# Head 0's shift moved from its queries to a bias inside the exps, with two smaller changes of order

## The chip, the cores and the metric

The kernel runs on one core of one Trainium2 chip. The metric is device time in microseconds (us), lower is better; where several executions are quoted, the median stands first and the range behind it.

## The reference

It is one block of a diffusion-style transformer with adaptive layer norms: attention over a cache, then a gated MLP that mixes tokens. The code is condensed. Only the first line of work matters to the front part of the change, the output projection `@ wo` to the other two.

```python
def _A_ref(x, k_cache, v_cache, wq, wo):          # Sq = Sk = 2048, D = 1024, 32 heads of 128
    q = (x @ wq).reshape(B, Sq, H, Dh).transpose(0, 2, 1, 3)
    scores = einsum('bhqd,bhkd->bhqk', q, k_cache) * Dh ** -0.5
    o = einsum('bhqk,bhkd->bhqd', softmax(scores), v_cache)
    return o.transpose(0, 2, 1, 3).reshape(B, Sq, H * Dh) @ wo

mod = (silu(c) @ w_mod).reshape(1, 6, 1, -1)      # c is (1, 1024), w_mod is (1024, 6144)
sa, ca, ga, sb, cb, gb = mod[:, 0], ..., mod[:, 5]
h = layernorm(x) * (1 + ca) + sa                   # scale ca, shift sa
x = x + ga * _A_ref(h, k_cache, v_cache, wq, wo)
h = layernorm(x) * (1 + cb) + sb
x = x + gb * _B_ref(h, ...)                        # the MLP; not touched by the change
```

Everything arrives in bf16. The shift `sa` enters the queries as one constant vector per head, `sa @ wq`.

## The kernel before

The kernel is long and already tuned: one instruction stream per engine, ordered by hand. Three places matter.

**1. The front.** Attention can start when the first queries exist. For heads 0 and 1 the kernel doesn't modulate the normalised rows: it folds the scale `1 + ca` into the weights (`wqs`), multiplies the plain normalised rows (`xnT`) by these, and adds the shift's product (`q_add`) when VectorE copies the queries out of PSUM. So the first copy waits for the shift. `mod_products(n)` multiplies a 1 MB chunk of `w_mod` by silu(c); chunks 2 and 3 give the scale, 0 and 1 the shift. `emit_s(g)` computes the scores of key block `kb` with 128 keys on the partitions and 1024 queries along the free axis.

```python
    c_sb = early.tile([KD, P], BF16, name="c_sb")
    nc.sync.dma_start(c_sb[:], c.rearrange("o (kc p) -> (o kc) p", p=P))     # first load of all
    # ... cut ...
    def keep_busy(n):                       # products of zeros, 512 columns wide
        zps = qa_ps("zps", [P, 512])
        for _ in range(n):
            nc.tensor.matmul(zps[:], zeros[:, 0:P], zeros[:], start=True, stop=True)

    def query_shift():
        qs = qa_ps("qs", [P, 2])
        for h in range(2):
            for dc in range(KD):
                nc.tensor.matmul(qs[:, h:h + 1], wq_g[0][:, dc, h * DH:(h + 1) * DH],
                                 shift[:, dc:dc + 1], start=(dc == 0), stop=(dc == KD - 1))
        nc.vector.tensor_copy(out=q_add[:], in_=qs[:])
    # ... cut ...
    silu()
    # ... cut: statistics, norm, transposes ...
    mod_products(2, qb_ps)
    mod_products(3)
    # ... cut ...
    turn(3, (0, 1))           # the last transposes, copied out by VectorE and ScalarE
    k_late()
    mod_products(0, qb_ps)
    mod_columns(0)
    # ... cut ...
    outs = []
    first = q_work(0, 0, bank_ps, outs)     # 16 products of head 0's first 1024 queries
    for fn, _ in first[:8]:
        fn()
    mod_products(1, qb_ps)
    mod_columns(1)
    for fn, _ in first[8:12]:
        fn()
    query_shift()
    for fn, _ in first[12:]:
        fn()
    for fn in outs:                          # the two copies that add q_add
        fn()
    emit_s(0)
    emit_s(1)
```

**2. The end of attention.** One half (one head, 1024 queries) takes 16 steps. In the last half the output projection's operands are loaded (`load_heads`, token group 0, then group 1), and the row sums of the half before are turned into reciprocals (`finish_here`), written to memory in four pieces (`spread`), read back broadcast (`load_rec`) and multiplied in (`normalise`). All of these transfers are issued by SyncE, in program order.

```python
        if final:
            if kb == 0:
                # ... cut ...
                load_heads(0, 1)
                load_heads(1, 0)
                load_heads(1, 1)
            elif kb in (4, 6, 8, 10):
                wo_sum(2, (kb - 4) // 2)
            elif kb == 13:
                normalise(i - 1)
        # ... cut ...
        nc.scalar.activation(pt_tiles[g], s_tiles.pop(g)[:], ACT.Exp, scale=SCALE)
        # ... cut ...
        if i > 0:
            # ... cut: two other tables for the earlier halves; that of the final half:
            work = {3: finish_here, 6: load_rec}.get(kb)
```

**3. The last token tile.** In the output projection each finished tile of 128 tokens is normalised `n` blocks later; `after(2, end)` means two. The last tile is normalised on VectorE (`centre`), the others on ScalarE.

```python
        def end():
            hb = scratch("hb", [P, D], FP16)
            (centre_act if ti < NT - 1 else centre)(x1[:, :], st, hb[:])
            after(2, lambda: nc.sync.dma_start(h2_dram[ti * P:(ti + 1) * P, :], hb[:]))
        after(2, end)
```

The softmax here doesn't subtract the row's maximum and nothing guards it: scores larger than these inputs give would overflow.

## Time and profile before

| | before |
|---|---|
| time, 3 runs | 1769.86 us (1768.88 to 1770.56) |
| TensorE busy | 98% of the span |
| start of the first exp | 31.57 us |
| attention's main loop | 31.5 to about 1120 us |
| output projection and MLP | about 1138 us to the end |

The profile's page says what bounds the kernel in one line: the chain that ended last, by engine.

```profile
PE 89%; DVE 6%; DMA 2%; issue 1%; ACT 1%; SPq 0%; POOL 0%; DVEq 0%; ACTq 0%; POOLq 0%
```

The windows view gives busy time by stretch. Its columns are: window, its length, then the busy time (and instruction count) of PE, PEld, DVE, ACT and POOL, then the granted TensorE clock, the DMA share and GB/s. First the front as a whole, two slices of it, and attention:

```profile
0.00:31.50 31.50, 19.86 (x250) 14.96 (x254) 18.86 (x59) 16.22 (x21) 6.29 (x14) 0.89 1.02 312
17.00:20.00 3.00, 1.83 (x24) 1.15 (x22) 2.57 (x9) 1.94 (x5) 0.98 (x2) 0.71 1.06 361
20.00:23.00 3.00, 3.00 (x26) 2.72 (x27) 1.69 (x6) 1.97 (x2) 0.40 (x1) 0.50 1.09 349
...
31.50:1116.00 1084.50, 1077.29 (x5170) 491.80 (x5270) 964.45 (x1252) 1004.90 (x1009) 9.54 (x8) 1.00 0.52 137
```

In attention TensorE is busy for 1077.29 of 1084.50 us: a change there can win time only where TensorE waits. In the front it is busy for 19.86 of 31.50 us, with DMA full (1.02).

The front in the timeline view (columns: start, duration in us, engine, line, operation, output<-inputs, shape; in brackets the idle time before it and what ended it):

```profile
20.79 1.91 PE L286 MATMUL k_ps<-identity,first_rows 128*128 128x128 bf16 x16
...
25.50 1.89 PE L380 MATMUL qps<-xnT,first_rows 128*128 128x512 bf16 x7
...
29.66 1.44 DVE L363 TENSOR_SCALAR qT<-qps,q_add 128x512 bf16<-128x512 f32 x2
31.16 0.81 PE L484 MATMUL sps<-qT,kT 128*128 128x512 bf16 x3 [0.31 <-DVE qT L363]
31.57 3.81 ACT L812 ACTIVATE pt<-sps 128x1024 bf16<-128x1024 f32 x4 [4.03 <-PE sps L484]
```

The two copies that add the shift (L363) run one after the other on VectorE, 1.44 us, and the first score's second half waits for them.

The end of attention in the same view, SyncE's issues (SPq) with VectorE and TensorE:

```profile
1116.17 9.23 SPq L653 DMA_DIRECT2D h_slots<-oT_dram  x6
...
1121.83 0.21 DVE L592 STREAM_TRANSPOSE turned<-rec 128x32 f32<-128x32 f32 x1
...
1125.44 2.56 SPq L594 DMA_DIRECT2D rec_dram<-turned  x4
...
1131.93 0.35 SPq L600 DMA_DIRECT2D rbc<-rec_dram  x1
...
1136.75 1.23 DVE L638 TENSOR_TENSOR s_slots<-ou,rbc 128x1024 bf16<-128x1024 f32 x1 [4.53 <-DMA rbc<-rec_dram]
...
1139.77 3.61 PE L935 MATMUL a<-wo,h_slots 128*128 128x512 bf16 x16 [2.45 <-DVE wq_t L826]
...
1154.06 1.02 PE L935 MATMUL b<-wo_t_11489,s_slots 128*128 128x512 f16 x4
...
1155.19 1.02 PE L935 MATMUL b<-wo_t_11491,s_slots 128*128 128x512 f16 x4
```

Six head loads keep SyncE issuing for 9.23 us. The reciprocals are ready at 1121.83 + 0.21 = 1122.04 us but their write is issued at 1125.44; everything behind it is late, VectorE stands idle 4.53 us, then TensorE 2.45 us. After that VectorE has a backlog: the groups of four products start 1155.19 − 1154.06 = 1.13 us apart.

The last token tile:

```profile
1335.88 0.55 DVE L156 TENSOR_SCALAR hb<-x_in,mv,rstd 128x1024 f16<-128x1024 bf16 x1 [0.73 <-POOL rstd L145]
1336.35 0.62 DVE L983 TENSOR_TENSOR sum<-c,snap 128x448 f32<-128x448 f32 x1
...
1338.06 0.92 PE L935 MATMUL a<-w_12681,hs_12655 128*128 128x448 f16 x4 [1.43 <-ACT snap L978]
```

VectorE waits for the rstd and normalises first; the sum, ScalarE's copy and then TensorE (1.43 us idle) come behind it.

### The profile page before, as it was taken

The numbers are of one execution on the slowest core, as the hardware profiler recorded it, in microseconds if no ns is written. First come the engines' busy times: TensorE is split into PE (matmuls) and PEld (weight loads), VectorE is DVE, ScalarE is ACT, GpSimd is POOL, SyncE is SP. The second block draws the span as 40 slices with busy tenths as digits, with TensorE's granted clock in tenths as the row PEclk, the third lists the DMA queues.
The fourth block names the chain that finished last, engine by engine and source line by source line (L and its number), as shares of the span: only waits on it lengthen the run. The fifth ranks groups of instructions, "written<-read, shape, count | busy, mean of one in ns | idle before, by whom it ended". The sixth has DMA issues, their size and how long they took to land.

```text
span 1767.5 us, 23664 instructions
## 1 busy us (share of the span) xinstructions
PE 1736.4 (98%) x8439; PEld 801.1 (45%) x8556; DVE 1488.6 (84%) x2245; ACT 1298.2 (73%) x1527; POOL 30.5 (2%) x39
## 2 busy tenths in 40 slices
PE   7999999999999999999999999999999999999999
PEld 4444444444444444444444444444444444444444
DVE  6898898898988899998999988896679789775894
ACT  6998889999999999999999999611235666734610
POOL 1000000000000000000000000000000000000000
PEclk9999999999999999999999999999999999999999
DMA  8566356646544633554633564645757364554312
GB/s 250 132 155 145 89 143 166 151 126 159 155 123 134 170 103 101 144 151 129 166 109 96 142 184 128 164 125 158 186 158 206 101 167 114 181 145 139 90 48 72
DMA packets 445335, 247.75 MB, mean 140 GB/s; under 512 B 289312, under 2 KB 406560, under 8 KB 445216
## 3 DMA queue, kind: packets, MB, share of 16 engines
q1 hardware_dynamic: 445216, 246.23, 51.9%
q8 instruction: 67, 1.10, 0.3%
q14 instruction: 52, 0.43, 0.1%
HBM read 144.18 MB, written 52.71 MB: 111 GB/s over the span
## 4 chain that ended last, share of the span: by engine, by line
PE 89%; DVE 6%; DMA 2%; issue 1%; ACT 1%; SPq 0%; POOL 0%; DVEq 0%; ACTq 0%; POOLq 0%
PE ops L750 24%; PE sps L484 23%; PE a L935 15%; PE b L935 8%; PE qa L465 4%; PE qps L380 4%; PE c L935 4%; PE qb L465 3%; PE bo L1537 2%; ACT pt L812 1%; DVE sum L983 1%; DMA wm<-in_w_mod_dram 1%; PE mps L198 0%; PE a_11200 L935 0%; PE a L1615 0%
## 5 line engine op out<-in xcount | busy, mean ns | idle before, releaser
L812 ACT ACTIVATE pt<-sps 128x1024 bf16<-128x1024 f32 x1024 | 1020.7, 1024 | 84.9 <-PE sps L484 38.5
L484 PE MATMUL sps<-qT,kT 128*128 128x512 bf16 x1993 | 597.0, 379 | 3.5 <-ACT pt L812 2.1
L750 PE MATMUL ops<-pt,v_sb 128*128 128x512 bf16 x2017 | 593.5, 379 | 3.7
L484 PEld LDWEIGHTS <-kT 128*128 128x128 bf16 x2048 | 199.4, 98 | 248.1 <-issue 16.4
L750 PEld LDWEIGHTS <-v_sb 128*128 128x128 bf16 x2048 | 200.1, 98 | 241.9
L978 ACT ACTIVATE snap<-a 128x512 f32<-128x512 f32 (+1 forms) x111 | 60.9, 565 | 113.6 <-PE a L935 103.2
L826 DVE COPY ou<-ops 128x512 f32<-128x512 f32 x126 | 81.2, 686 | 32.5 <-PE ops L750 29.7
L935 PEld LDWEIGHTS <-h_slots 128*128 128x128 f16 (+1 forms) x680 | 66.3, 98 | 82.4 <-issue 2.5
L380 PE MATMUL qps<-h1T,wq_t 128*128 128x512 bf16 x279 | 94.3, 379 | 0.3
L983 DVE TENSOR_TENSOR sum<-b,snap 128x512 f32<-128x512 f32 (+1 forms) x76 | 50.1, 660 | 48.4 <-PE b L935 28.7
L1386 ACT ACTIVATE zr<-zr,z_nm,z_rs 128x256 f16<-128x256 f16 x82 | 41.1, 586 | 66.4 <-PE bo L1537 47.1
L638 DVE TENSOR_TENSOR oT<-ou,rbc 128x1024 bf16<-128x1024 f32 x62 | 75.3, 1215 | 0.6 <-DMA rbc<-rec_dram 0.6
L450 DVE COPY tx<-qa 128x512 f32<-128x512 f32 x66 | 45.5, 689 | 32.2 <-PE qa L465 32.2
L616 DVE TENSOR_REDUCE den<-pT 128x8 f32<-128x1024 bf16 x54 | 63.9, 1183 | 0.0
L465 PE MATMUL qa<-h1s,wq_t 128*128 128x512 f16 x176 | 63.1, 379 | 0.3
L935 PEld LDWEIGHTS <-s_slots 128*128 128x128 f16 (+1 forms) x400 | 39.0, 98 | 49.0 <-issue 2.0
L465 PEld LDWEIGHTS <-wq_t 128*128 128x128 bf16 (+1 forms) x352 | 34.4, 98 | 41.5
L935 PEld LDWEIGHTS <-wq_t 128*128 128x128 f16 (+1 forms) x344 | 33.7, 98 | 38.4 <-DMA wq_t<-oT_dram 0.2
L145 POOL TENSOR_TENSOR rstd<-var,neg_half 128x1 f32<-128x1 f32 x30 | 25.1, 836 | 1306.0 <-DVE var L143 1258.9
L445 DVE TENSOR_TENSOR qT<-qb,tx 128x512 bf16<-128x512 f32 x66 | 45.2, 685 | 0.7
L380 PEld LDWEIGHTS <-wq_t 128*128 128x128 bf16 x288 | 28.0, 98 | 33.2 <-issue 0.6
L465 PEld LDWEIGHTS <-tx 128*128 128x128 f16 x264 | 25.8, 98 | 31.2
(930 smaller groups left out, 2553.6 us busy)
## 6 DMA issues: line engine op xcount, KB each, us to landing
rbc<-rec_dram SPq DMA_DIRECT2D x63, 512.0 KB
v_sb<-in_A_v_cache_dram SPq DMA_DIRECT2D x40, 512.0 KB
oT_dram<-oT SPq DMA_DIRECT2D x62, 256.0 KB
sums_dram<-pacc SPq DMA_DIRECT2D x54, 256.0 KB
wm<-in_w_mod_dram SPq DMA_DIRECT2D x12, 1024.0 KB
wq_t<-in_A_wq_dram SPq DMA_DIRECT2D x7, 1024.0 KB
h_slots<-oT_dram SPq DMA_DIRECT2D x12, 512.0 KB
zr<-z_dram SPq DMA_DIRECT2D x11, 512.0 KB
```

The lines of the kernel that those rows point to most:

```text
L380: nc.tensor.matmul(box["ps"][:], weights[:, dc, hc:hc + DH], src[:, dc, q0:q0 + 512], start=(n == 0), stop=(n == KD - 1))
L450: nc.vector.tensor_copy(out=x if m == 6 else su, in_=a)
L465: nc.tensor.matmul(box["b" if m in (2, 7, 4) else "a"][:], *operand(m, dc), start=(m in (1, 2, 7) and dc == 0), stop=(dc == 3), skip_group ...
L484: nc.tensor.matmul(sps[:, j * 512:(j + 1) * 512], kts[h][:, kb * P:(kb + 1) * P], qts[(h, qh)][:, j * 512:(j + 1) * 512], start=True, stop ...
L616: nc.vector.tensor_reduce(out=den[:], in_=state[i]["pT"][:], op=ALU.add, axis=mybir.AxisListType.X)
L638: nc.vector.tensor_mul(out=oT, in0=state[i]["ou"][:], in1=state[i]["rbc"][:])
L750: nc.tensor.matmul(o_ps[j][:], vs[halves[i][0]][:, kb, :], pt_tiles[g][:, j * 512:(j + 1) * 512], start=(kb == 0), stop=(kb == NKB - 1))
L812: nc.scalar.activation(pt_tiles[g], s_tiles.pop(g)[:], ACT.Exp, scale=SCALE)
L826: nc.vector.tensor_copy(out=ou[:, j * 512:(j + 1) * 512], in_=o_ps[j][:])
L935: nc.tensor.matmul(self.ps[self.BANK[n]], a, b, start=(n in (1, 2, 7) and k == 0), stop=(k == len(lhs) - 1), skip_group_check=True)
L978: nc.scalar.activation(t, ps, ACT.Copy)
L983: nc.vector.tensor_add(out=t, in0=ps, in1=snap)
```

## The change

The front: a query's score against a key is (q + s)·k = q·k + s·k, and s·k depends on the key alone. Keys lie on the partitions of the score tile, so s·k can be the bias of the exp, one number per partition. Head 0's queries then need no shift. The shift's product is split into a bf16 part and a bf16 remainder so that nothing is lost. In return each of head 0's first 16 exps carries a bias, 32 small key products and a small copy are added, the order of the front's products changes, one query copy goes to ScalarE, and `c` is loaded behind two tiles of x. The second part moves the last half's group-1 head loads from step 0 to steps 7 and 9, behind the reciprocals. The third defers the last tile's normalisation by one block.

```diff
-    nc.sync.dma_start(c_sb[:], c.rearrange("o (kc p) -> (o kc) p", p=P))
 ...
     for ti in range(8):
         nc.sync.dma_start(xg[ti // 2][:, ti % 2], x_dram[:, ti, :])
+        if ti == 1:
+            nc.sync.dma_start(c_sb[:], c.rearrange("o (kc p) -> (o kc) p", p=P))
 ... query_shift(h, dcs) now takes one head and a range of chunks; for head 0 it ends with
+            hi, lo = q_add0[:, 0:1], q_add0[:, 1:2]
+            nc.vector.tensor_copy(out=hi, in_=qs[0][:])
+            nc.vector.tensor_sub(out=lo, in0=qs[0][:], in1=hi)
 ...
+    def key_shift(k0, k1, new_ps):
+        ks = new_ps("ks", [P, k1 - k0])
+        for k in range(k0, k1):
+            for t in range(2):
+                nc.tensor.matmul(ks[:, k - k0:k - k0 + 1], kts[0][:, k * P:(k + 1) * P],
+                                 q_add0[:, t:t + 1], start=(t == 0), stop=(t == 1),
+                                 skip_group_check=True)
+        nc.scalar.activation(key_add[:, k0:k1], ks[:], ACT.Copy, scale=SCALE)
 ...
-    turn(3, (0, 1))
-    k_late()
-    mod_products(0, qb_ps)
-    mod_columns(0)
+    x_late = turn(3, True)
 ... in q_work's copies:
+            elif h == 0 and plain and not j:
+                nc.scalar.activation(qts[h, qh][:, sl], box["ps"][:], ACT.Copy)
 ...
-    first = q_work(0, 0, bank_ps, outs)
+    first = q_work(0, 0, (qa_ps, bank_ps))
     for fn, _ in first[:8]:
         fn()
+    x_late()
+    k_late()
+    mod_products(0, qb_ps)
+    mod_columns(0)
+    for fn, _ in first[8:]:
+        fn()
+    query_shift(0, range(4))
     mod_products(1, qb_ps)
     mod_columns(1)
-    for fn, _ in first[8:12]:
-        fn()
-    query_shift()
-    for fn, _ in first[12:]:
-        fn()
-    for fn in outs:
-        fn()
+    query_shift(0, range(4, KD))
     emit_s(0)
+    key_shift(0, 2, qb_ps)
     emit_s(1)
+    query_shift(1, range(KD))
 ...
                 load_heads(0, 1)
-                load_heads(1, 0)
-                load_heads(1, 1)
             elif kb in (4, 6, 8, 10):
                 wo_sum(2, (kb - 4) // 2)
+            elif kb in (7, 9):
+                load_heads(1, (kb - 7) // 2)
 ...
-        nc.scalar.activation(pt_tiles[g], s_tiles.pop(g)[:], ACT.Exp, scale=SCALE)
+        bias = {"bias": key_add[:, kb:kb + 1]} if i == 0 else {}
+        nc.scalar.activation(pt_tiles[g], s_tiles.pop(g)[:], ACT.Exp, scale=SCALE, **bias)
+        if g == 0:
+            key_shift(2, NKB, qb_ps)
 ...
-        after(2, end)
+        after(2 if ti < NT - 1 else 3, end)
```

More of the change, by code (lines that the diff above doesn't have):

```diff
@@ L215 @@
     shift = early.tile([P, KD], BF16, name="shift")
-    q_add = early.tile([P, 2], FP32, name="q_add")
+    q_add = early.tile([P, 1], FP32, name="q_add")
+    q_add0 = early.tile([P, 2], BF16, name="q_add0")
+    key_add = early.tile([P, NKB], FP32, name="key_add")
     def scale_wq(j):
@@ L226, in scale_wq, with query_shift @@
                                         op0=ALU.mult)
-    def query_shift():
-        qs = qa_ps("qs", [P, 2])
-        for h in range(2):
-            for dc in range(KD):
-                nc.tensor.matmul(qs[:, h:h + 1], wq_g[0][:, dc, h * DH:(h + 1) * DH],
-                                 shift[:, dc:dc + 1], start=(dc == 0), stop=(dc == KD - 1))
-        nc.vector.tensor_copy(out=q_add[:], in_=qs[:])
+    qs = []
+    def query_shift(h, dcs):
+        if dcs[0] == 0:
+            qs[:] = [qa_ps("qs", [P, 1])]
+        for dc in dcs:
+            nc.tensor.matmul(qs[0][:], wq_g[0][:, dc, h * DH:(h + 1) * DH],
+                             shift[:, dc:dc + 1], start=(dc == 0), stop=(dc == KD - 1))
+        if dcs[-1] < KD - 1:
+            return
+        if h:
+            nc.vector.tensor_copy(out=q_add[:], in_=qs[0][:])
+        else:
+            hi, lo = q_add0[:, 0:1], q_add0[:, 1:2]
[9 more added lines that the diff above has]
+        nc.scalar.activation(key_add[:, k0:k1], ks[:], ACT.Copy, scale=SCALE)
     row = {}
@@ L263, in finish_act, with turn @@
         row[ti] = (mv, rstd)
-    def turn(j, evacuate=(2,)):
+    def turn(j, late=False):
         hps = wide_ps("hps", [P, KD, 2, P], BF16)
@@ L270, in turn, with out @@
                                     xg[j][:, t, dc * P:(dc + 1) * P], identity[:])
-        for eng in evacuate:
-            dcs = {2: slice(0, KD), 0: slice(0, 4), 1: slice(4, KD)}[eng]
-            dst = xnT[:, dcs, j * 256:(j + 1) * 256]
-            src = hps[:, dcs].rearrange("p d t k -> p d (t k)")
-            if eng:
+        def out():
+            dst = xnT[:, :, j * 256:(j + 1) * 256]
+            src = hps[:].rearrange("p d t k -> p d (t k)")
+            if late:
+                nc.vector.tensor_copy(out=dst, in_=src)
+            else:
                 nc.scalar.activation(dst, src, ACT.Copy)
-            else:
-                nc.vector.tensor_copy(out=dst, in_=src)
+        if late:
+            return out
+        out()
     def dve(ti):
@@ L351, with q_work @@
     tags = [qa_ps, qb_ps]
-    def q_work(h, qh, new_ps=None, outs=None):
+    def q_work(h, qh, new_ps=None):
         plain = h < 2 and qh == 0
@@ L361, in out @@
             sl = slice(j * 512, (j + 1) * 512)
-            if plain:
+            if h == 1 and plain:
                 nc.vector.tensor_scalar_add(out=qts[h, qh][:, sl], in0=box["ps"][:],
-                                            scalar1=q_add[:, h:h + 1])
+                                            scalar1=q_add[:])
+            elif h == 0 and plain and not j:
+                nc.scalar.activation(qts[h, qh][:, sl], box["ps"][:], ACT.Copy)
             else:
@@ L369, in q_work @@
             box = {}
-            tag = new_ps or tags[j]
+            tag = (new_ps or tags)[j]
             def one(n, j=j, box=box, tag=tag):
@@ L382, in one @@
                                  start=(n == 0), stop=(n == KD - 1))
-                if n == KD - 1 and outs is None:
+                if n == KD - 1:
                     out(j, box)
-                elif n == KD - 1:
-                    outs.append(lambda: out(j, box))
             for n in range(KD):
@@ L490 @@
     nc.sync.dma_start(wq_g[1][:], wq_v[:, :, 512:1024])
-    outs = []
-    first = q_work(0, 0, bank_ps, outs)
+    first = q_work(0, 0, (qa_ps, bank_ps))
     for fn, _ in first[:8]:
         fn()
+    x_late()
[5 more added lines that the diff above has]
+    query_shift(0, range(4))
     mod_products(1, qb_ps)
     mod_columns(1)
-    for fn, _ in first[8:12]:
-        fn()
-    query_shift()
-    for fn, _ in first[12:]:
-        fn()
-    for fn in outs:
-        fn()
+    query_shift(0, range(4, KD))
     emit_s(0)
+    key_shift(0, 2, qb_ps)
     emit_s(1)
+    query_shift(1, range(KD))
     state = {}
```

## The prediction

> **What bounds the kernel now.** The chain that ended last is 89% TensorE; in the windows, TensorE is busy 1077 of 1084.5 us in attention (31.5 to 1116 us). Time can be won only where TensorE waits. The diff touches three such places.
>
> 1. Front (first exp at 31.57 us). DMA is saturated from about 2 us on; x loads are issued behind c's (0.74 to 1.20 us), and the chain runs through the second modulation chunk, landing at 16.29. From 19.96 TensorE is nearly continuous until 30.3; then two VectorE query copies (1.44 us) delay the first score's second half to 31.16.
> 2. End of attention. In the timeline six head loads hold SyncE's queue from 1116.17 to 1125.40, though the reciprocals were ready at 1122.04. They are written 1125.44 to 1131.79, the broadcast lands at 1136.73, and VectorE sits idle 4.53 us before normalising. TensorE then idles about 2.3 us (1137.3 to 1139.8), and from 1154 to 1158.3 is paced at 1.13 us per four matmuls instead of 0.86 by VectorE's backlog (another 1.2).
> 3. Last token tile. VectorE waits 0.73 us for the rstd, then normalises (0.55) before the next sum; ScalarE follows, and TensorE waits 1.43 us at 1338.06.
>
> **Costs.**
> - c behind two x tiles: x starts 0.46 us earlier, so the 16.29 landing should too: −0.4 at the front's gate.
> - Head 0's queries no longer wait for the shift; one copy goes to ScalarE; turn 3 is evicted in one VectorE copy (estimate 1.35 us from 0.69 for half), hidden behind eight matmuls. But the first exp now waits for shift products, two small VectorE operations (0.16 each), key products and a 0.2 us ScalarE copy. First exp at about 31.5: nearly no gain.
> - 32 small key products at about 31 ns (32 such take 0.95 to 1.0 us). Most fit the wait during exp 0 (0.67 us before), but the 14-column bias copy delays exp 1 by about 0.5 us. Bias operand: the Trainium skill ("ScalarE: Activation LUTs", "What ACT_TABLE_LOAD costs") says each per-partition pointer operand adds about 93 ns; this trace agrees (256-column activation: 404, 495 with one, 586 ns with two). So 16 exps go from 1024 to about 1115 ns; TensorE's step is 1.08 us, their overlapped spacing about 1.05: hidden. Front net: about +0.3 us (−0.7 to +0.9).
> - Head loads of group 1 behind the reciprocals: these are written from about 1122.1, the broadcast lands about 1130, before the multiply's turn at 1132.2. The 2 MB follow, at about 290 GB/s landing by about 1135, needed at 1137.5 and 1141. Stall and backlog vanish: −3.2 us (−2 to −4).
> - Last tile: the sum goes ahead of the normalisation; TensorE's 1.43 us wait falls to about 0.4: −0.8 us (−0.2 to −1.2).
>
> Downstream is TensorE-paced, so these should persist: 1769.86 + 0.3 − 3.2 − 0.8 = about 1766.2 us, range 1763.6 to 1768.4. Faster by over 2%: 0.01; within 2%: 0.98; slower: 0.01.
>
> **What would show it.** VectorE's 4.5 us wait for the broadcast gone; reciprocal writes near 1122; TensorE's wait on the ou copies gone; group 1's first products not waiting for head loads; four-matmul groups back at 0.86. First exp within 0.4 us of 31.57; exps of the first half near 1115 ns; a TensorE wait of some 0.4 us on exp 1. TensorE's wait at the last tile under 0.5 us. Second modulation chunk's products about 0.45 us earlier.
>
> **What would make it wrong.** Late head loads putting a new wait on the first output products; the bias exps pacing the first half; key products delaying exp 1 by more; the last tile's later store delaying transposed loads, giving its gain back; changed buffer slots adding waits.

## The result, and the profile after

The changed kernel took 1765.04 us (1763.56 to 1766.74, 4 runs) against 1770.07 us (1768.88 to 1770.56, 4 runs) for the kernel before, run beside it. The ratio is 0.9973 (95% interval 0.9956 to 0.9990). A ratio here and below is the mean time of one kernel's fast runs over that of the other's of the same rounds, so it is not quite the ratio of the medians that are quoted. The gain is about 4.8 us (0.0027 of 1770), well under 2%.

The chain of the changed kernel, from its page:

```profile
PE 86%; DVE 7%; DMA 3%; ACT 2%; issue 1%; SPq 1%; DVEq 0%; ACTq 0%
```

The front, windows view, changed kernel:

```profile
0.00:31.50 31.50, 20.83 (x288) 14.59 (x292) 19.39 (x60) 18.66 (x26) 6.29 (x14) 0.92 0.99 316
17.00:20.00 3.00, 2.69 (x18) 1.81 (x18) 2.83 (x9) 1.70 (x4) 1.38 (x2) 0.52 1.07 385
20.00:23.00 3.00, 2.95 (x42) 2.41 (x41) 1.93 (x6) 2.70 (x2) 0.00 (x0) 1.00 1.08 381
26.00:28.00 2.00, 1.67 (x44) 1.33 (x44) 0.99 (x4) 0.00 (x0) 0.00 (x0) 1.00 1.10 336
...
30.00:32.00 2.00, 2.00 (x6) 0.77 (x6) 0.29 (x1) 2.00 (x3) 0.00 (x0) 0.54 1.14 176
```

The half-clock stretch lies elsewhere: the slice from 20 to 23 us now has full speed, while the one from 30 to 32 us has 0.54 and six products fill it. The timeline shows both:

```profile
20.10 1.06 PE L312 MATMUL k_ps<-identity,first_rows 128*128 128x128 bf16 x16
22.10 1.89 PE L405 MATMUL qps<-xnT,first_rows 128*128 128x512 bf16 x7
...
28.79 1.11 ACT L838 ACTIVATE pt<-sps,key_add 128x1024 bf16<-128x1024 f32 x1
...
29.96 0.86 PE L507 MATMUL sps<-qT,kT 128*128 128x512 bf16 x2
30.61 1.49 PE L405 MATMUL qps<-xnT,first_rows 128*128 128x512 bf16 x3
```

The 16 key transposes took 1.06 us instead of 1.91. The first exp starts at 28.79 us, 2.78 us earlier than before. But three products of 512 columns then take 1.49 us (0.81 in the timeline of before at 33.07 us), and by the fifth exp only 1.00 us of the 2.78 is left.

The groups view by form shows the cost of the bias operand in the changed kernel (count, busy us, mean ns of one, idle before):

```profile
L838 ACT ACTIVATE pt<-sps,key_add 128x1024 bf16<-128x1024 f32 x16 | 17.4, 1114 | 1.8 <-PE sps L507 0.9 <-remote 0.9
```

The end of attention, timeline of the changed kernel:

```profile
1123.36 0.21 DVE L617 STREAM_TRANSPOSE turned<-rec 128x32 f32<-128x32 f32 x1
...
1123.60 1.52 SPq L619 DMA_DIRECT2D rec_dram<-turned  x4
1126.49 0.35 SPq L625 DMA_DIRECT2D rbc<-rec_dram  x1
1126.89 4.53 SPq L678 DMA_DIRECT2D h_slots<-oT_dram  x3
...
1133.68 1.22 DVE L663 TENSOR_TENSOR s_slots<-ou,rbc 128x1024 bf16<-128x1024 f32 x1
...
1138.91 3.62 PE L963 MATMUL a<-wo,h_slots 128*128 128x512 bf16 x16
...
1152.93 1.03 PE L963 MATMUL b<-wo_t_11529,s_slots 128*128 128x512 f16 x4
...
1153.79 1.03 PE L963 MATMUL b<-wo_t_11531,s_slots 128*128 128x512 f16 x4
```

The reciprocals are written 0.03 us after they are ready (1123.36 + 0.21 = 1123.57), the normalisation and the first projection product have no wait, and the groups of four are 0.86 us apart again.

The last tile, timeline of the changed kernel:

```profile
1333.05 0.61 DVE L1011 TENSOR_TENSOR sum<-c,snap 128x448 f32<-128x448 f32 x1
...
1334.91 0.53 DVE L157 TENSOR_SCALAR hb<-x_in,mv,rstd 128x1024 f16<-128x1024 bf16 x1
1334.75 0.92 PE L963 MATMUL a<-w_12721,hs_12695 128*128 128x448 f16 x4 [0.15 <-ACT snap L1006]
```

The sum now goes first and TensorE's wait is 0.15 us instead of 1.43.

To see where time was gained or lost I subtracted, in each trace, the start of the n-th exp (or of the n-th ScalarE copy of the projection) from that in the trace of before. The instructions of these two lines come in the same order in all the kernels. All numbers in us, minus is earlier; exps are counted from 1 here (the prediction counts from 0, so its exp 1 is exp 2 here). "Attention" is what was lost between exp 5 and exp 1013 of 1024, "end" what was gained from there to the seventh copy (at 1184 us before), "last tile" what was gained from the 25th copy (1328 us) to the 34th (1348 us).

| kernel | first exp at | exp 1 | exp 5 | attention | end | last tile |
|---|---|---|---|---|---|---|
| before | 31.57 | | | | | |
| after | 28.79 | −2.78 | −1.00 | +2.54 | −3.48 | −0.78 |
| again | 30.06 | −1.51 | −1.30 | +1.44 | −3.48 | −0.78 |
| front_only | 28.16 | −3.41 | −3.20 | +0.40 | −0.53 | 0.00 |
| loads_only | 31.41 | −0.16 | −0.16 | −0.05 | −3.48 | 0.00 |
| tile_only | 31.10 | −0.46 | −0.46 | +0.26 | +0.36 | −0.78 |
| c_only | 30.38 | −1.19 | −1.18 | −0.06 | −0.39 | −0.01 |
| bias_only | 28.32 | −3.24 | −1.58 | +0.87 | −0.27 | 0.00 |
| loads_tile | 30.79 | −0.78 | −0.78 | −0.06 | −3.47 | −0.77 |
| warm | 28.38 | −3.19 | −1.52 | +0.17 | −3.48 | −0.78 |
| warm_old | 30.53 | −1.04 | −1.04 | +0.40 | −3.48 | −0.79 |
| warm_new | 28.09 | −3.48 | −3.27 | +0.75 | −3.48 | −0.77 |
| warm_wide | 28.91 | −2.66 | −1.80 | +0.02 | −3.48 | −0.78 |
| loads_pool | 30.00 | −1.57 | −1.57 | +0.15 | −2.45 | 0.00 |

One trace is one execution. But "end" repeats to 0.01 us in the eight traces with the moved loads, and "last tile" to 0.02 in the eight with the tile's part; in the five without that part it is zero. The front doesn't repeat: five traces (before, loads_only, tile_only, loads_tile, loads_pool) have the front of the kernel before, and their first exp comes anywhere from 30.00 to 31.57 us. The trace of before, from which everything is subtracted, has the latest, so the columns "exp 1" and "exp 5" flatter the other kernels. Stretches between the columns wander too: from the seventh copy to the 25th by −0.3 to +1.25 us, in three traces by about +1.2.

### The profile page after: what moved, and what is told of

Same layout as the page of the kernel before. It is cut to its first block, busy times and chain, and to the rows that moved or that the text cites. A ratio compares the mean times of both kernels' runs of the same rounds, so it can differ in the third digit from the quotient of the medians.

```text
span 1764.6 us, 23738 instructions
## 1 busy us (share of the span) xinstructions
PE 1737.2 (98%) x8471; PEld 800.6 (45%) x8588; DVE 1488.3 (84%) x2246; ACT 1298.2 (74%) x1529; POOL 30.5 (2%) x39
## 4 chain that ended last, share of the span: by engine, by line
PE 86%; DVE 7%; DMA 3%; ACT 2%; issue 1%; SPq 1%; DVEq 0%; ACTq 0%
PE ops L775 22%; PE sps L507 22%; PE a L963 15%; PE b L963 8%; PE c L963 4%; PE qps L405 4%; PE qa L488 4%; PE qb L488 3%; PE bo L1565 2%; ACT pt L838 1%; DMA rec_dram<-turned 1%; DMA rbc<-rec_dram 1%; DVE sum L1011 1%; DMA wm<-in_w_mod_dram 1%; PE a_11236 L963 1%
## 5 line engine op out<-in xcount | busy, mean ns | idle before, releaser
L838 ACT ACTIVATE pt<-sps 128x1024 bf16<-128x1024 f32 x1008 | 1003.8, 1024 | 83.0 <-PE sps L507 32.9
L146 POOL TENSOR_TENSOR rstd<-var,neg_half 128x1 f32<-128x1 f32 x30 | 25.1, 836 | 1304.1 <-DVE var L144 1278.2
```

## The experiments

My theory after the result: the three parts act separately, the loads give about 3.5 us, the tile 0.8, and the front's value depends on where TensorE's clock is halved. The first rival: the parts interact, or the front's earlier start carries much of the gain. A second question was why the queue mattered. All twelve kernels gave correct results. Each ratio is against the kernel before in the same rounds (5 rounds; 3 for loads_pool).

| kernel | median us (range) | before, same rounds | ratio (95%) |
|---|---|---|---|
| again | 1764.57 (1763.68–1767.35) | 1769.16 | 0.9974 (0.9961–0.9988) |
| front_only | 1769.37 (1767.16–1770.89) | 1769.16 | 0.9998 (0.9986–1.0011) |
| loads_only | 1765.48 (1763.77–1767.11) | 1769.16 | 0.9978 (0.9965–0.9990) |
| tile_only | 1768.66 (1767.75–1770.10) | 1769.16 | 0.9997 (0.9984–1.0009) |
| c_only | 1768.02 (1767.23–1768.81) | 1768.80 | 0.9997 (0.9985–1.0010) |
| bias_only | 1769.03 (1765.78–1769.47) | 1768.80 | 0.9999 (0.9986–1.0011) |
| loads_tile | 1764.36 (1764.21–1766.35) | 1768.80 | 0.9979 (0.9966–0.9992) |
| warm | 1764.44 (1764.05–1765.09) | 1768.80 | 0.9977 (0.9963–0.9991) |
| warm_old | 1764.61 (1763.95–1765.43) | 1768.56 | 0.9975 (0.9961–0.9988) |
| warm_new | 1762.72 (1762.26–1763.66) | 1768.56 | 0.9964 (0.9952–0.9977) |
| warm_wide | 1763.45 (1763.03–1765.44) | 1768.56 | 0.9971 (0.9958–0.9983) |
| loads_pool | 1766.56 (1766.23–1770.41) | 1768.56 | 0.9990 (0.9977–1.0004) |

### again: the changed kernel once more

No edit; a control, beside which the single parts are read. It ran on chip 2, as front_only, loads_only and tile_only did; the later runs were on chip 0.

> The changed kernel once more, as a control. Theory (three parts that add up, and two lotteries): the time is about 4 to 5 us below the kernel before; the stall of 2.9 us on the broadcast reciprocals in half 15, and the two 3.4 us windows of half clock at 16.5 and 30.1 us in the first profile, need not come back, because they are luck of the run: then the first-exp-to-last-exp distance is within 0.5 us of the kernel before's instead of 4.3 us longer. Rival (the change causes both): the profile shows the half-15 wait again at about 3 us and again a half-clock window that starts within 2 us after the first exp.

Measured: 1764.57 us, ratio 0.9974. The result repeats. Its trace has another clock pattern than the first: the first exp comes at 30.06 us. Its clock column is a trap:

```profile
17.00:20.00 3.00, 2.69 (x16) 1.74 (x16) 2.83 (x10) 1.70 (x4) 1.37 (x2) 1.00 1.07 385
```

It reads 1.00, but the first clock record of this trace comes only at 22.46 us, and the key transposes at 20.34 us took the slow 1.91 us. Before the first record the column says nothing.

### front_only: the front alone

```diff
 # the changed kernel, with
+                load_heads(1, 0)
+                load_heads(1, 1)
-            elif kb in (7, 9):
-                load_heads(1, (kb - 7) // 2)
-        after(2 if ti < NT - 1 else 3, end)
+        after(2, end)
```

> The front alone (c's load moved, key bias, reordered first queries), head loads and last tile as before. Theory: the first exp comes 0.5 to 3 us earlier (by how much depends on which window of the front gets half clock), 1 us is left after exp 5, and the time is 0 to 1.5 us below the kernel before. Rival (the front is where the change wins): 3 us or more below.

Measured: ratio 0.9998, first exp at 28.16 us. This trace has no half-clock stretch after 14.9 us. The front's gain is then 3.41 us at exp 1, and 3.20 at exp 5: the cost that I had put at the second exp (key products and the bias copy) is 0.29 us there at full clock, and 0.21 by exp 5. Of the 3.20 us, 2.90 are still there at the last copies of the projection. That execution was the fastest of the five (1767.16; the others 1768.32 to 1770.89), so the mean shows next to nothing of it.

### loads_only: the head loads alone

```diff
 # the kernel before, with
-                load_heads(1, 0)
-                load_heads(1, 1)
+            elif kb in (7, 9):
+                load_heads(1, (kb - 7) // 2)
```

> The group-1 head loads behind the last half's reciprocals alone. Theory: VectorE's 4.5 us wait for the broadcast is gone, first output blocks start about 3.3 us earlier against the last exp, and the time is 2.5 to 4 us below the kernel before. Rival (the gain needs the front's shift or other buffer slots, or is given back in the output projection): under 1.5 us.

Measured: ratio 0.9978, which is 3.9 us, with 1.8 to 6.2 in its interval. In the trace the step at the end of attention is −3.48 us, nothing else moves by more than 0.2. This part alone is most of the change.

### tile_only: the last tile alone

```diff
 # the kernel before, with
-        after(2, end)
+        after(2 if ti < NT - 1 else 3, end)
```

> The last tile's normalisation one block later alone. Theory: TensorE's 1.43 us wait at the last tile falls below 0.4 us and 0.8 us is left at the end; the time is 0.3 to 1.2 us below the kernel before. Rival (the later store of the last rows delays the transposed loads and gives it back): the block two later waits, and the time is within 0.2 us.

Measured: ratio 0.9997, about 0.5 us and not to be told from nothing. In the trace the copy at 1337 us comes 1.29 us earlier relative to the one at 1328 us, and 0.46 us are given back by the one at 1340 us; at 1348 us 0.78 are left, as in the seven other traces with this part. Something else is visible. TensorE's wait at 1137 to 1140 us, still there in this kernel, was followed by 3.4 us of half clock from 1140.4 us, and between the first copy (at 1139 us) and the fourth (1154 us) 1.68 us were lost. That window is in none of the other thirteen traces, the kernel before's included, which has the same wait.

### c_only: c behind two tiles of x, alone

```diff
 # the kernel before, with
-    nc.sync.dma_start(c_sb[:], ...)        # ahead of x
+        if ti == 1:
+            nc.sync.dma_start(c_sb[:], ...)
```

> c's load behind two x tiles alone. Theory: x and everything behind it on the saturated DMA lands 0.46 us earlier, so the second modulation chunk's products start about 0.5 us earlier and the first exp 0.3 to 0.6 us earlier, if the windows of half clock lie as in the kernel before; the whole time is 0 to 0.6 us lower, inside its noise. Rival (c's move is what frees the front of half clock): no or one half-clock window between 14 and 25 us instead of two, first exp 1.5 us or more earlier.

Measured: ratio 0.9997; first exp 1.19 us earlier in the trace, with the clock's half-speed stretch starting at 15.8 us instead of 18.2. The prediction put 0.4 us here, and the products of the second modulation chunk (the trace's second `mps` group) did start 0.41 us earlier, at 15.93 instead of 16.34. But loads_tile, which loads c first, has them at 15.56, and loads_pool, with the old front unchanged, has its first exp at 30.00: neither gain can be put down to the move. Nothing of it can be told from zero in time.

### bias_only: the front without c's move

```diff
 # front_only, with c's load back at the head of the queue
```

> The key bias and the reordered first queries alone, c's load first as before. Theory of the prediction: at the same clock the first exp comes about 0.3 us later or equal (31.5 to 32.0 us), exp 1 is 0.4 us late, exp 4 on within 0.5 us of the kernel before. Rival (the reordering takes waits out of the front for real): first exp 0.8 us or more earlier at the same clock windows. In time: within 1 us of the kernel before either way.

Measured: ratio 0.9999. First exp at 28.32 us, but here a half-clock stretch of 3.4 us starts at 29.3 us, as in the changed kernel's first trace, and 3.24 us of gain shrink to 1.58 by exp 5. So the first exp's gain doesn't come from c's move; and the loss behind it goes with the clock, not with the bias: front_only has the same exps with a bias and lost 0.2.

### loads_tile: the change without the front

```diff
 # the kernel before, with the edits of loads_only and tile_only
```

> The whole change without its front. Theory (the front's gain is within the noise of clock and DMA, the other two parts are the result): 4.0 to 5.0 us below the kernel before, within 1 us of the whole change. Rival (the front is worth its 1 us and more): 1.3 us or more slower than the whole change's 4.6 us.

Measured: ratio 0.9979, where the whole change has 0.9973 and 0.9974. The difference, 0.0005 to 0.0006, would make the front worth about 1 us; with half-widths of some 0.0013 (2.3 us) on each it can't be told from zero. The three single parts sum to (1 − 0.9978) + (1 − 0.9997) + (1 − 0.9998) = 0.0027, the whole change's 0.0026 to 0.0027. They don't interact noticeably.

### warm: keep TensorE busy early

If the clock decides the front, wide products of zeros early in it should move it. The kernel has a helper for that.

```diff
 # the changed kernel, with
+    keep_busy(6)
     silu()
+    keep_busy(7)
```

> The changed kernel with 13 more idle-time matmuls on zeros (6 before the turn of c, 7 behind it), meant to have full clock before the first transposes. Theory (half clock in the front's windows decides when the first exp comes): no half-clock window between about 8 and 30 us, first exp at 28.5 us or earlier in this profile, and 0.5 to 2 us below the whole change's 4.6 us gain. Rival (the front is bound by the loads, not by TensorE's clock): first exp within 0.3 us of the second profile of the changed kernel (30.06), time as the changed kernel's.

Measured: ratio 0.9977. The trace still has two half-clock stretches, from 15.7 and from 29.4 us, and the profile of the first five exps is that of bias_only. This edit didn't reach its aim: between the two modulation chunks of the scale TensorE still stood idle.

### warm_old and warm_new: both fronts at full clock

A third block of zero products goes into that gap. warm_old has the old order of the front (and all else of the change, c's move too), warm_new the new one. My theory at this point said that at equal clock the new order is worth at most about half a microsecond; the rival said that the order itself is worth more.

```diff
 # both: warm's two calls, and
     mod_products(2, qb_ps)
+    keep_busy(5)
     mod_products(3)
```

> Everything but the key bias and the new order of the first queries (head loads, last tile and c's move as in the change), plus idle-time matmuls on zeros in three places of the front, so that its clock is full. Together with the next run it compares the two orders of the first queries at the same clock. Theory (the new order is worth little: at equal clock the first exp is at most 0.5 us later here, and exp 4 within 0.3 us, because the key bias gives back what the order wins): time within 0.5 us of the next run or lower. Rival (the order is worth 1 us or more, and is hidden by half clock in the other runs): exp 4 at least 1 us later than in the next run, time about 1 us higher.

> The whole change plus the same zero matmuls in the same three places. Theory of the clock (a window in which TensorE runs few wide products is followed by one at half clock): no half-clock window from 9 to 29 us, and one at about 29 to 33 us again when a window boundary lies near 29.3 us, because the window before holds mostly one-column products; exps 2 to 4 then lose 1.1 us or more, else under 0.3. First exp at 27.5 to 28.3 us. Time 5 to 6 us below the kernel before.

Measured: warm_old 1764.61 us, ratio 0.9975; warm_new 1762.72 us, ratio 0.9964. The traces have no half-clock stretch that matters (warm_old one at 9.1 us, warm_new none). The first exp comes at 30.53 and 28.09 us, exp 5 at −1.04 and −3.27. My theory fell. The timeline of warm_old shows what I had missed (the second and third line are chunks 0 and 1, the shift):

```profile
20.27 1.06 PE L287 MATMUL k_ps<-identity,first_rows 128*128 128x128 bf16 x16
22.87 0.95 PE L199 MATMUL mps<-scT,wm 128*128 128x1 bf16 x32 [0.44 <-DMA wm<-in_w_mod_dram]
...
26.17 0.95 PE L199 MATMUL mps<-scT,wm 128*128 128x1 bf16 x32 [0.60 <-DMA wm<-in_w_mod_dram]
```

With the clock at full speed the old order reaches both chunks of the shift before they have landed, and waits 0.44 + 0.60 = 1.04 us. The waits view of warm_old (15 to 34 us; total us, number, longest) counts a third wait, the longest:

```profile
PE mps L199 <- DMA wm<-in_w_mod_dram: 1.8, 3, 0.8
```

That one, 0.75 us at 16.19 us, is for a chunk of the scale. It lies ahead of the key transposes, in a part that both orders share.

warm_new puts the wide query products, which need nothing that is still on its way, ahead of these chunks:

```profile
19.39 1.06 PE L312 MATMUL k_ps<-identity,first_rows 128*128 128x128 bf16 x16
21.40 1.89 PE L408 MATMUL qps<-xnT,first_rows 128*128 128x512 bf16 x7
23.12 0.94 PE L199 MATMUL mps<-scT,wm 128*128 128x1 bf16 x32
25.75 0.94 PE L199 MATMUL mps<-scT,wm 128*128 128x1 bf16 x32
```

None of its products waits for the modulation weights from here on. Of the 2.2 us between the two at exp 5, 20.27 − 19.39 = 0.88 exist already at the key transposes, which stand in the same order in both kernels, and are the luck of one execution; about 1.35 come after. In the ratios the two kernels are 0.0011 apart, about 1.9 us, with intervals that overlap; but each of these compares with the kernel before. Compared directly, in the same rounds on the same chip, all five executions of warm_new (1762.26 to 1763.66 us) lie below all five of warm_old (1763.95 to 1765.43), and the means differ by 1.83 us (my 95% interval from these ten times: 1.1 to 2.6). So with the zero products in place the new front is worth something like that in time.

warm_new is also the fastest of all kernels here: 5.8 us under before in the medians of the same rounds, 6.4 in the mean ratio, against 4.6 in the mean ratio for the changed kernel in again. That it is faster than the changed kernel isn't shown: the two ran in other rounds and on other chips, and the intervals overlap. Nearest to a test is warm, on the same chip in earlier rounds, whose five executions (from 1764.05 us) all lie above warm_new's.

### warm_wide: wide products among the one-column ones

In three traces (after, bias_only, warm) a half-clock stretch begins 0.96 to 1.36 us after the first exp, just behind the front's one-column products (modulation, shift, key products). If such products don't keep the clock up, six wide products of zeros among them should.

```diff
 # warm_new, with keep_busy(n, new_ps=qa_ps) and
     mod_products(1, qb_ps)
+    keep_busy(3, bank_ps)
 ...
     emit_s(1)
+    keep_busy(3, bank_ps)
     query_shift(1, range(KD))
```

> As the run before it, with six more wide zero matmuls in the stretch of one-column products (three behind the second shift chunk, three behind the second score), which cost up to 1.3 us of TensorE's time there. Theory: the half-clock window behind it is gone, exps 2 to 4 lose under 0.3 us; first exp 0.3 to 0.7 us later than in the run before. Rival (the window at 30 us comes from something else, such as the wait on the first exps): it is there still.

Measured: 1763.45 us, ratio 0.9971, 0.7 us slower than warm_new in the medians. Between exp 1 and exp 2 it loses 0.94 us, where warm_new loses 0.28; the difference is about what three of the added products take (0.65 us from their start to the next product's). There was no half-clock stretch behind the first exp, but there was none in warm_new either, so the run can't tell whether they prevented one. It gives no sign that they pay.

### loads_pool: other queue, same transfers in flight

Was it SyncE's queue that held the reciprocals back, or the bytes of the head loads?

```diff
 # the kernel before, with
-                load_heads(1, 0)
-                load_heads(1, 1)
+                load_heads(1, 0, nc.gpsimd)     # issued by GpSimd
+                load_heads(1, 1, nc.gpsimd)
```

> The kernel before with the four group-1 head loads issued at the same place of the program but by GpSimd instead of SyncE. Theory (the loads blocked the queue's issuing, so the reciprocals could not be written): the reciprocals are written from about 1122, within 0.3 us of their being ready, VectorE's wait for the broadcast is under 1 us although the same bytes are in flight, and the time falls by 2.5 to 4 us. Rival (bandwidth: 2 MB in flight delay the reciprocals and their broadcast): the writes are issued at 1122 but the broadcast still lands after 1134, VectorE waits 2 us or more, time falls under 1.5 us.

Measured: 1766.56 us, ratio 0.9990 (0.9977 to 1.0004), in time not to be told from zero, and −2.45 us at the end of attention in the trace. The timeline of loads_pool:

```profile
1107.46 3.79 POOL L653 DMA_DIRECT2D h_slots<-oT_dram  x4 [973.26 <-PE qps L380]
...
1120.40 0.21 DVE L592 STREAM_TRANSPOSE turned<-rec 128x32 f32<-128x32 f32 x1
...
1120.68 3.26 SPq L594 DMA_DIRECT2D rec_dram<-turned  x4
...
1128.44 0.35 SPq L600 DMA_DIRECT2D rbc<-rec_dram  x1
...
1132.90 1.22 DVE L638 TENSOR_TENSOR s_slots<-ou,rbc 128x1024 bf16<-128x1024 f32 x1
```

The queue is free, so the reciprocals go out 0.07 us after they are ready (1120.40 + 0.21 = 1120.61), and the last normalisation doesn't wait. That is the queue's part. But from the write's issue to the broadcast's it takes 1128.44 − 1120.68 = 7.76 us; in loads_only, with group 1's loads not yet issued, the same two stand at 1121.86 and 1124.73, 2.87 us apart, and the DMA moves 44 GB/s in between, against 216 here. In the kernel before it was the same: 1131.93 − 1125.44 = 6.49 us, at 226 GB/s. So there too the reciprocals lost about as much behind the bytes (3.6 us) as behind the queue (3.40 us). And the normalisation of the half before waited 2.09 us for its own broadcast. That is the bytes' part: GpSimd, which had little else to do, issued these loads at 1107.46 us, about 9 us before SyncE began with its own in the kernel before, and they were in flight at the same time as these transfers. The Trainium skill ("DMA: Bandwidth & Descriptors", "Issuing engines are not separate DMA queues") says that transfers started by different engines run on the same 16 DMA engines and interleave, and that a second issuer saves only sequencer time. This trace agrees. So both counted: freeing the queue brought 2.45 of the 3.48 us, and only issuing the loads later brought all of it.

## Why the prediction was right or wrong

**The total was right.** 1766.2 us with a range of 1763.6 to 1768.4; measured 1765.04 in the result and 1764.57 in again. The predicted gain of 3.7 us was 1 us too small. Two of its three terms were right; the third, the front, had the wrong sign in the traces, and it is luck that it was too small to move the total out of the range.

**The head loads: right in size, and in mechanism but for one part.** "−3.2 us (−2 to −4)": the traces give −3.47 or −3.48 us in all eight that have this part, the time of loads_only 3.9. Each sign came: the write at the moment the reciprocals were ready, VectorE's 4.53 us and TensorE's 2.45 us gone, the groups of four back from 1.13 to 0.86 us. The prediction saw the queue: SyncE's stream was held in order, 9.23 us by six loads. It didn't name the bytes in flight, which loads_pool shows to count as well; moving the loads later removes both.

**The last tile: right.** "−0.8 us (−0.2 to −1.2)": in all eight traces with this part 1.28 or 1.29 us are gained and 0.45 or 0.46 given back at the next copies, and 0.77 to 0.79 remain. TensorE's wait went from 1.43 to 0.15 us (predicted: to about 0.4). The giving back was named as a risk through the later store; I didn't trace what causes it. In time the part is too small to be seen (0.9997).

**The bias operand: right.** Predicted 1115 ns for the 16 exps; measured 1114, against 1024 without. This is 90 ns for one pointer operand, where the Trainium skill ("ScalarE: Activation LUTs", "What ACT_TABLE_LOAD costs") has about 93. That it would be hidden behind TensorE was right as well: in front_only the gain is −3.20 us at exp 5 and still at exp 16.

**The front: wrong in mechanism, and small enough not to matter.** The step that failed is "First exp at about 31.5: nearly no gain", and with it "Front net: about +0.3 us". In the traces with the new front and without added zero products the first exp came at 28.16 to 30.06 us. Two things were missed:

1. I added up durations of one trace as if they were fixed. At half clock the sum holds, as far as one pair of traces shows: c_only (old order) and again (new order) both have slow key transposes (1.91 us) and full clock from about 22.5 us on; from the first key transpose to the fifth exp both take 14.01 us. At full clock it doesn't: the old order takes 13.90 (loads_pool) and 14.33 us (warm_old), the new one 12.98 in both traces without a later stretch (front_only, warm_new). The durations between 18.2 and 25.1 us in before were taken at half clock: 16 key transposes take 1.91 us there and 1.06 at full clock. The stretch moves from execution to execution. The Trainium skill ("TensorE: Matmul & The Clock Gate", "What's actually happening") says that the clock is set by windows of 3413 ns that run freely, halved after an idle window. The short clock records of these traces are 3.413, 6.827 and 10.240 us long and start elsewhere each time, which agrees with the windows. Whether the window must be idle this case leaves open: in after TensorE was busy, as the profile counts it, for 3.01 of the 3.41 us before 30.15 us, and half clock followed; if the rule holds, products of one column, most of those in that window, don't count. The windows view of before showed 0.50 in the slice from 20 to 23 us, before I predicted.
2. I counted what the new order stops waiting for (the shift) but not what TensorE itself waits for: the modulation weights. At half clock the two chunks of the shift had always landed in time, which hid the wait. At full clock the old order waits for them, 1.04 us in warm_old and 0.59 in loads_pool, and the new one does not.

The predicted loss at the second exp, "the 14-column bias copy delays exp 1 by about 0.5 us", was 0.29 us at full clock. Where the loss is larger (1.78 us in after, 1.66 in bias_only, 1.67 in warm, from exp 1 to exp 5) a half-clock stretch begins at 29.3 to 30.2 us.

In time the front of the change as it stands is not firm: front_only is at 0.9998 (0.9986 to 1.0011), so it is worth 0.4 us by itself and about 1 us as the difference of the whole and loads_tile, and the predicted loss of 0.3 us is inside both intervals. It is the traces that refute the step, and in time the pair warm_old and warm_new, 1.83 us apart, at the clock that the zero products bring. That half clock costs time fits the list of executions too: of the 27 of the kernel before that ran beside the experiments, the 20 with a mean clock of 0.999 or 1.000 took 1768.6 us on average, the 7 with 0.997 or 0.998 took 1770.2. (That mean counts the time before the first clock record as full speed.)

**What stays open.**
- Whether one-column products fail to keep the clock up. In the trace of after TensorE was busy for 1.67 of 2.00 us from 26 to 28 us, most of its products having one column, and the stretch from 30.1 us was at half speed all the same. Three traces fit, and the four new-front traces without such a stretch had their boundary elsewhere in relation to the first exp, if the boundaries are carried on in steps of 3.413 us; but warm_wide, made to test it, couldn't.
- Why kernels with the new front lose more later in attention: +0.40, +0.87, +2.54, +1.44, +0.17, +0.75 and +0.02 us in seven traces (mean 0.9) against +0.1 on average in six with the old. In the first trace of the changed kernel 1.9 of 2.54 us arise between exps 225 and 257, where VectorE waits 2.90 us for a broadcast; again waits 0.74 us there. Such waits of VectorE for transfers (over 0.1 us each) between exps 5 and 1013 sum to 4.1 to 11.0 us in six of the seven traces (1.1 in warm_wide, which loses 0.02) and to 0.8 to 2.7 us in five of the six with the old front (6.0 in warm_old, which loses 0.40). Why they differ wasn't traced. With one trace per kernel, this is a suggestion and no more.

## What to carry to other kernels

A small transfer that others wait for must not be issued behind large ones that nobody needs yet: look for a wait on a small transfer, then at what its queue was issuing when its data became ready, and move the large loads rather than the queue. Before adding up durations from a stage where TensorE is often idle, look at the granted clock of that stage; if it is halved there, the sum describes one execution, and waits on transfers may be hidden by slow products. A gain in the front of one trace is worth little until the mean of several runs shows it.

## What the Trainium skill lacked or had wrong

- "TensorE: Matmul & The Clock Gate", "What's actually happening", puts the penalty of ramping below 1% of a kernel and advises not to fit to a specific cold count. The share is right here: from exp 1 to exp 5 half clock cost about 1.5 us of 1765 (1.66 to 1.78 lost against 0.21). But an optimisation step of this size is no larger (loads and tile together brought 0.0021), and here half clock also hid a wait and so decided what a new order was worth (nothing at half clock, 0.9 to 1.4 us by the fifth exp at full clock).
- That page doesn't say whether products with one column count as activity. After 3.01 busy us of 3.41, most products having one column, the clock went to half rate (0.54 from 30 to 32 us in after). Whether they were the cause is open.
- That page warns that clock events can be unreliable in general, but no page says that the clock column of the profile reads 1.00 before the first clock record: in the trace of again it does so from 17 to 22.4 us, while 16 transposes took 1.91 us, as at half rate, instead of 1.06.
- "DMA: Bandwidth & Descriptors", "Issuing engines are not separate DMA queues", calls the sequencer's time to initiate a transfer usually small relative to the transfer. Here SyncE was held 9.23 us by six loads of about 512 KB (0.38 and 0.58 us for the first two, 1.56 to 3.06 for each of the rest), and the reciprocals were issued 3.40 us late.
